# Blockwise attention with a routed MoE behind it: pages taken through the experts in an order found on the chip

## The chip, the cores and the metric

The kernel runs on 1 core of a Trainium2 chip. The metric is the device time of one execution in microseconds (us). One core has TensorE (PE, matrix multiplications; its weight loads are shown apart, as PEld), VectorE (DVE), ScalarE (ACT), GpSimd (POOL) and SyncE (SP, which here only issues transfers), each with its own instruction queue worked off in order, and 16 DMA engines that carry all transfers. SBUF is the memory the engines work on, PSUM the one that PE writes its results to.

## What is computed

Causal attention in blocks of 64, then a mixture of experts in which each token goes to one expert and no token is dropped:

```python
B, H, S, D = (8, 8, 576, 64)            # attention; x becomes N = 4608 rows of 512
N, D, E, F = (4608, 512, 8, 1024)       # MoE
...
scores = scale * np.matmul(q, k.transpose(0, 1, 3, 2))
mask = block_i >= block_j
attn = np.exp(scores - max) / sum
x = np.matmul(attn, v)                  # to [B * S, H * D]
...
expert_idx = np.argmax(x @ w_gate, axis=1)
gate_w = the softmax of x @ w_gate at expert_idx
for e in range(E):                      # the tokens of expert e
    y[e's tokens] = np.maximum(x[e's tokens] @ w1[e], 0.0) @ w2[e]
return gate_w[:, None] * y
```

The inputs are drawn at random from a fixed seed. How many tokens each expert gets is known only on the chip.

## The kernel before

**Attention** runs over 32 pairs of heads (`p`; four pairs are one batch `b`). The order of PE, ACT and POOL is written out by hand in the loop over `p`; DVE's and SP's order is found by the scheduler. A turn of the loop works on several pairs at once: POOL casts `q` and `k` of pair p+2 to 16 bits (`cast`), PE transposes them into the PSUM buffers `tp` (`trans`, L199, L201) and DVE copies them into `qkT` (L203, L205); PE makes the scores of pair p+1 (L230), ACT their exponentials `pt`; PE multiplies pair p's `pt` by `v` (`attend`, L261); DVE adds blocks of `pt` in `sums` (three instructions, the third is L243); PE makes the denominators (L284) and, in `finish`, transposes the result and multiplies it by the gate weights in one go (L304 with the denominators, L308), and DVE multiplies by the reciprocal into the rows `x16` and the logits `lgp` (L314 to L326). All transposes, denominators, finishes and the rank matmuls below share two PSUM buffers `tp`.

**Routing.** `route(b)` stands behind the finish of a batch's fourth pair. DVE sums the logits (L333), finds the largest and the one-hot `oh` of the expert (to L364); PE ranks the tokens in six matmuls (L367, L371), which stand in PE's queue directly behind finish; DVE then works out each token's row (`slot`) in `xsorted`, a table in DRAM of 43 pages of 128 rows, in which every page belongs to one expert (L378 to L409), and keeps count, pages in use and each expert's open page. `scatter(b, j)` writes a fifth of a batch's rows to their slots with an indirect DMA (L425), spread over the next batch's pairs. The weights (16 MB in fp16, `wall`) are loaded in 16 DMAs between pairs. `em_all` collects what is needed to say which expert each page has.

**Seam.** After the last route POOL issues five scatters, and DVE and PE work out `emap`, the expert of each of the 43 pages.

**MoE** goes through the pages in their order in the table. SP loads page T+4 (`mload`), PE reads the expert's number of that page into a register (`values_load`, L499). Per page PE does the first layer (`m1`, eight matmuls of 512 columns, L520, in which the register picks the weights), the transposes of the next page (`mtx`, four), those of the hidden layer of the page before (`mth`, eight, L532), and the second layer of the page before that (`m2`, eight matmuls, L542); DVE copies the transposes to SBUF, ACT applies relu and the gate, POOL writes the rows out with an indirect DMA (L546). The MoE's buffers are pools of their own, opened after those of attention are closed.

Of the kernel before, what the change touches and what calls it, by code (L numbers as in the profile page):

```python
# [22 lines left out]
def kernel(  # L23
# [69 lines left out]
    emap = consts.tile([1, NP], I32)  # L93
# [41 lines left out]
    with tc.tile_pool(name="ld", bufs=2) as ld, \  # L135
# [3 lines left out]
         tc.tile_pool(name="ptp", bufs=2) as ptp, \  # L139
# [4 lines left out]
         tc.tile_pool(name="t_ps", bufs=2, space=bass.MemoryType.PSUM) as t_ps:  # L144
# [186 lines left out]
        def route(b):  # L331
# [3 lines left out]
            x16 = st.pop(("x16", b))  # L335

            def small(name, w=E):
                return rp.tile([128, w], F32, name=name)

            def wide(name):  # L340
                return rp.tile([128, 5, E], F32, name=name)

            def over_j(t):
                return t.unsqueeze(1).to_broadcast([128, 5, E])

            def over_e(t):
                return t.unsqueeze(2).to_broadcast([128, 5, E])

# [4 lines left out]
            ex = wide("ex")  # L353
            nc.scalar.activation(ex, d, AF.Exp)
# [10 lines left out]
                                    in1=over_e(m2)[0:64, 4, :], op=ALU.is_equal)  # L365
            rk_ps = t_ps.tile([128, 6 * E], F32, name="tp")
# [54 lines left out]
        def scatter(b, j):  # L421

            slot, x16 = st["slot", b], st["x16", b]
            m = 128 if j < 4 else 64
            ins = nc.gpsimd.indirect_dma_start(  # L425
                out=xsorted[:, :],
                out_offset=bass.IndirectOffsetOnAxis(ap=slot[0:m, j:j + 1], axis=0),
                in_=x16[0:m, j, :], in_offset=None)
            apart("rows", ins)

        with tc.manual_schedule(engines={ET.PE, ET.Activation, ET.Pool}):
# [12 lines left out]
            for p in range(PAIRS):  # L444
# [13 lines left out]
                if p >= HP and p % HP < 3:  # L458
                    scatter(p // HP - 1, p % HP)
# [18 lines left out]
        for j in range(5):  # L478
            scatter(B - 1, j)
        with tc.manual_schedule(engines={ET.PE, ET.Activation}):  # L480
            em = rp.tile([128, 1], F32, name="em")
            nc.vector.reduce_sum(out=em, in_=em_all, axis=AX.X)
            em_ps = t_ps.tile([1, 128], F32, name="tp")
            nc.tensor.transpose(em_ps, em, ident32)
            nc.vector.tensor_scalar(emap, em_ps[:, 0:NP], -1.0, None, op0=ALU.add)
            nc.vector.tensor_single_scalar(emap, emap, E - 1, op=ALU.bitwise_and)  # L486

    with tc.tile_pool(name="xs", bufs=8) as xsp, \
         tc.tile_pool(name="m_sb", bufs=3) as m_sb, \
         tc.tile_pool(name="hp_ps", bufs=2, space=bass.MemoryType.PSUM) as hp_ps, \  # L490
         tc.tile_pool(name="yp_ps", bufs=2, space=bass.MemoryType.PSUM) as yp_ps, \
         tc.tile_pool(name="tt_ps", bufs=1, space=bass.MemoryType.PSUM) as tt_ps:
        pg = {}

        def mload(T):
            xs = xsp.tile([128, ROW], I32, name="xs")
            nc.sync.dma_start(out=xs, in_=xsorted[T * 128:T * 128 + 128, :])  # L497
            pg["xs", T] = xs
            pg["e", T] = nc.values_load(  # L499
                emap[0:1, T:T + 1], engines=[ET.PE], min_val=0, max_val=E - 1,  # L500
                skip_runtime_bounds_check_because="the low three bits of an integer")

        def mtx(T):
            ps = tt_ps.tile([128, 512], F16, name="xps")
# [10 lines left out]
        def m1(T):  # L515
            xT = pg.pop(("xT", T))
            hp = hp_ps.tile([128, F], F32, name="hp")
# [10 lines left out]
        def mth(T):  # L528
            h = pg.pop(("h", T))
            ps = tt_ps.tile([128, F], F16, name="hps")  # L530
            for f in range(8):
                nc.tensor.transpose(ps[:, f * 128:f * 128 + 128],  # L532
                                    h[:, f:F:8], ident16)
            hT = m_sb.tile([128, F], F16, name="hT")
            nc.vector.tensor_copy(hT, ps)  # L535
            pg["hT", T] = hT

        def m2(T):
            hT, xs = pg.pop(("hT", T)), pg.pop(("xs", T))
            yp = yp_ps.tile([128, Dm], F32, name="yp")  # L540
# [11 lines left out]
        with tc.manual_schedule(engines={ET.PE, ET.Activation}):  # L552
            for T in range(4):
# [43 lines left out]
```

## Time and profile before

| | |
|---|---|
| time, median of 3 runs | 531.01 us (529.99 to 533.31) |
| the profiled execution | 528.41 us |
| its span in the trace | 526.5 us |
| mean granted clock of TensorE | 0.933 |
| busy: PE, DVE, ACT, POOL | 446.2, 265.5, 205.9, 190.8 us |

The span runs from the first to the last instruction that the profiler recorded; 1.9 us of the execution's time lie around it. The views of the trace name an instruction by its line in the kernel (L520), its engine, its operation, and by tiles, "out<-in". In a timeline a row gives the start in us from the span's beginning, the duration, and in brackets how long the engine had been idle before and who released it; neighbours of one kind are drawn together (x8 is eight instructions). "issue" is idle time in which the engine waited for nothing that the profile shows. A granted clock of 1.00 is TensorE's full speed.

### The profile page before, as it was taken

Reading aid. Unit: us, or ns where it says so; the run is one execution under the profiler, and the core shown is the slowest. Engines: PE = TensorE matmul, PEld = TensorE weight load, DVE = VectorE, ACT = ScalarE, POOL = GpSimd, SP = SyncE. Lnnn points to the kernel's source line nnn. Section 1 sums busy time; section 2 is a strip of 40 time slices with the busy share of each in tenths; the row PEclk is TensorE's granted clock in tenths of the full one; section 3 lists DMA queues with packets and bytes.
Section 4 is the critical chain, followed back from the end, with each engine's and each line's share of the span. In section 5 each row is a group of like instructions: output and inputs, shape, how many; then the busy total and the mean of one; then the engine's idle time right before and its main releaser. Section 6 shows DMA issues by size and latency. Waiting matters only on the chain. (4 is left out here: it accounts for less than half of the span.)

```text
span 526.5 us, 11426 instructions
## 1 busy us (share of the span) xinstructions
PE 446.2 (85%) x4005; PEld 271.3 (52%) x4005; DVE 265.5 (50%) x745; ACT 205.9 (39%) x319; POOL 190.8 (36%) x379
## 2 busy tenths in 40 slices
PE   2996987896996996996996970699999999999991
PEld 1564655564664664664663650355555555555550
DVE  1567466778777677667867752122222222322220
ACT  2453443353453453452452520144334434434431
POOL 7433174354462463553552503022222222222221
PEclk9999899899898997997997995699999999999996
DMA  4689987678498586789585562212222232322200
GB/s 123 200 231 231 239 198 195 159 186 189 119 209 209 115 210 156 155 199 213 131 212 102 105 128 68 59 60 100 102 82 91 81 101 82 119 76 90 82 18 0
DMA packets 85589, 71.40 MB, mean 136 GB/s; under 512 B 52640, under 2 KB 80032, under 8 KB 83488
## 3 DMA queue, kind: packets, MB, share of 16 engines
q1 hardware_dynamic: 78000, 39.71, 28.9%
q0 software_dynamic: 7536, 30.98, 24.8%
q8 instruction: 34, 0.56, 0.4%
q14 instruction: 19, 0.16, 0.1%
HBM read 67.56 MB, written 21.71 MB: 170 GB/s over the span
## 5 line engine op out<-in xcount | busy, mean ns | idle before, releaser
L233 ACT ACTIVATE pt<-s 128x1024 f32<-128x1024 f32 x96 | 94.7, 1022 | 82.7 <-PE s L230 70.6
L261 PE MATMUL o<-pt,v 128*64 128x320 f32 (+3 forms) x768 | 102.6, 421 | 1.9 <-DMA v<-in_v_dram 1.9
L546 POOL DMA_INDIRECT out_dram<-y,xs x43 | 42.3, 984 | 149.8 <-ACT y L545 149.8
L509 DVE COPY xsT<-xps 128x512 f16<-128x512 f16 x43 | 18.3, 425 | 137.7 <-PE xps L506 95.8
L520 PE MATMUL hp<-wall,xsT 128*128 x344 | 83.0, 385 | 2.6 <-DVE xsT L509 2.6
L542 PE MATMUL yp<-wall,hT 128*128 x344 | 81.1, 379 | 0.0
L261 PEld LDWEIGHTS o<-pt,v 128*64 128x64 f32 x768 | 57.3, 152 | 44.5 <-issue 20.4
L203 DVE COPY qkT<-tp 128x512 f16<-128x512 f16 x64 | 43.9, 686 | 62.4 <-PE tp L201 55.9
L525 ACT ACTIVATE h<-hp 128x1024 f16<-128x1024 f32 x43 | 44.0, 1023 | 67.9 <-PE hp L520 66.8
L235 POOL MEMSET pt<- 64x128 f32 x128 | 23.6, 199 | 128.8 <-ACT pt L233 90.6
L187 POOL CAST qk<-qk 128x512 f16<-128x512 f32 x64 | 53.0, 851 | 12.8 <-DMA qk<-in_k_dram 6.2
L520 PEld LDWEIGHTS <-xsT 128*128 128x128 f16 x344 | 34.0, 99 | 43.8 <-issue 3.0
L308 PE MATMUL tp<-wgi,oT 128*128 128x144 f32 x320 | 55.0, 305 | 0.0
L425 POOL DMA_INDIRECT xsorted<-x,slot x40 | 41.5, 1038 | 34.2 <-DVE emap L486 14.2
L545 ACT ACTIVATE y<-yp,xs 128x512 f32<-128x512 f32 x43 | 29.5, 687 | 60.0 <-PE yp L542 60.0
L542 PEld LDWEIGHTS <-hT 128*128 128x128 f16 x344 | 32.2, 99 | 30.7
L265 ACT COPY oT<-o 128x256 f32<-128x256 f32 x64 | 25.7, 402 | 50.8 <-PE o L261 50.8
L308 PEld LDWEIGHTS tp<-wgi,oT 128*128 128x128 f32 x320 | 42.7, 190 | 2.9
L239 DVE TENSOR_TENSOR acc<-pt 128x896 f32<-128x896 f32 x32 | 35.0, 1092 | 18.0 <-issue 10.6
L230 PE MATMUL s<-qkT 64*128 64x512 f16 (+4 forms) x320 | 36.4, 321 | 2.5 <-DVE qkT L203 1.8
L535 DVE COPY hT<-hps 128x1024 f16<-128x1024 f16 x43 | 29.7, 692 | 7.8 <-PE hps L532 4.8
L199 PE MATMUL tp<-ident,qk 128*128 128x128 f16 x256 | 26.3, 227 | 8.0 <-POOL qk L187 8.0
(107 smaller groups left out, 489.6 us busy)
## 6 DMA issues: line engine op xcount, KB each, us to landing
wall<-in_moe_w_dram POOLq DMA_DIRECT2D x16, 1024.0 KB, 9.9
qk<-in_q_dram SPq DMA_DIRECT2D x32, 256.0 KB
qk<-in_k_dram SPq DMA_DIRECT2D x32, 256.0 KB
v<-in_v_dram SPq DMA_DIRECT2D x64, 128.0 KB
xs<-xsorted SPq DMA_DIRECT2D x43, 129.0 KB
xsorted<-fill SPq DMA_DIRECT2D x4, 516.0 KB
xsorted<-fill SPq DMA_DIRECT2D x3, 645.0 KB
xsorted<-fill SPq DMA_DIRECT2D x1, 1548.0 KB
```

Of the source, the lines that this page charges most:

```text
L187: nc.gpsimd.tensor_copy(h16[:, n, 0:4].rearrange("p c h d -> p h c d"), qk[:, n].rearrange("p h (c d) -> p h c d", c=4))
L203: nc.vector.tensor_copy(qkT[:, n, 0:512].rearrange("d (p c) -> d p c", c=4), ps[:, 0:512].rearrange("d (c p) -> d p c", c=4))
L230: nc.tensor.matmul(out=sp[:, h, o:o + w], lhsT=qkT[r, 1, c * 128:c * 128 + 128], rhs=qkT[r, 0, q0:q0 + w], start=True, stop=True)
L233: nc.scalar.activation(pt[:, :, t * 512:t * 512 + 512], sp, AF.Exp, scale=scale)
L239: nc.vector.tensor_tensor(out=acc[:, :, 0:448], in0=pt[:, :, 128:576], in1=pt[:, :, 576:1024], op=ALU.add)
L261: nc.tensor.matmul(out=o[h * 64:h * 64 + 64, q0 - lo:hi - lo], lhsT=vt[r, c, h, :], rhs=src, start=(c == 0), stop=(c == last), skip_group_ ...
L308: nc.tensor.matmul(out=ps[:, m * 144:m * 144 + 144], lhsT=oT[:, i * 128:i * 128 + 128], rhs=wgi[:, hp, :], start=True, stop=True, skip_gro ...
L425: ins = nc.gpsimd.indirect_dma_start(out=xsorted[:, :], out_offset=bass.IndirectOffsetOnAxis(ap=slot[0:m, j:j + 1], axis=0), in_=x16[0:m, ...
L520: nc.tensor.matmul(out=hp[:, half * 512:half * 512 + 512], lhsT=xT[:, c * 128:c * 128 + 128], rhs=weight(T, 2 * c + half), start=(c == 0), ...
L525: nc.scalar.activation(h, hp, AF.Relu)
L542: nc.tensor.matmul(out=yp, lhsT=hT[:, f * 128:f * 128 + 128], rhs=weight(T, 8 + f), start=(f == 0), stop=(f == 7))
L546: ins = nc.gpsimd.indirect_dma_start(out=out[:, :], out_offset=bass.IndirectOffsetOnAxis(ap=xs[:, 257:258], axis=0), in_=y, in_offset=None ...
```

## The change

The change has three parts.

- **Routing is split.** `choose(b)`, DVE's part up to `oh`, stays behind finish. `route(b)` (the exponential on ACT, the rank matmuls on PE and the rest of DVE's work) moves into the next pair, between its last scores and its denominators. Scatters move with it, two in each of the next two pairs' turns and one in the third; batch 6's fifth goes out after the loop.
- **The order of the pages.** After batch 6 `closed` marks the pages that are full, or whose expert has gone on to another page. `first_places` and `orders` number them with matmuls against a triangle of ones and put the first ten of them, page numbers and experts, into `order1`. The other 33 places get their pages in `order2`; their experts are known when batch 7 is routed (`last_experts`, `last_order`).
- **MoE begins before batch 7 is routed.** Its PSUM buffers are those of attention (`s`, `o0`, `o1`, `tp`), its SBUF buffers take the place of `pt`. Loads of the first ten places don't wait for batch 7's scatters. SP reads the page's number into a register for each load and runs five places ahead; PE reads the expert's number in `mtx`, one page ahead. `route(7)`, its scatters and the last experts stand behind m1 of place 1, `last_order` behind m1 of place 3.

```diff
-        def route(b):
+        def choose(b):
             lg = rp.tile([128, 5, E], F32, name="lg")
...
+            st["d", b] = d
+
+        def route(b):
+            d, x16, oh = st.pop(("d", b)), st.pop(("x16", b)), ohs[b % 2]
+            ex = wide("ex")
+            nc.scalar.activation(ex, d, AF.Exp)
             rk_ps = t_ps.tile([128, 6 * E], F32, name="tp")
...
+        def closed():
+            cur, hit = small("cur"), small("hit")
+            opn, cl = small("opn", 1), small("cl", 1)
+            nc.vector.scalar_tensor_tensor(out=cur, in0=lastA, scalar=-1.0, in1=pages,
+                                           op0=ALU.add, op1=ALU.add)
+            nc.vector.tensor_scalar(hit, cur, page_f, 0.0, op0=ALU.is_equal, op1=ALU.add,
+                                    accum_out=opn)
+            nc.vector.scalar_tensor_tensor(out=cl, in0=page_f, scalar=used, in1=opn,
+                                           op0=ALU.is_lt, op1=ALU.is_gt)
...
+        def orders():
+            on, fst, rest, em_h = st.pop("first")
+            ps = t_ps.tile([128, 3 * FIRST], F32, name="tp")
+            nc.tensor.matmul(out=ps[0:1, 0:FIRST], lhsT=page_h, rhs=on, start=True, stop=True,
+                             skip_group_check=True)
+            nc.tensor.matmul(out=ps[0:1, FIRST:2 * FIRST], lhsT=em_h, rhs=on, start=True,
+                             stop=True, skip_group_check=True)
...
+            nc.vector.tensor_copy(order1, ps[0:1, 0:2 * FIRST])
...
-                if p >= HP and p % HP < 3:
-                    scatter(p // HP - 1, p % HP)
+                if p > HP and p % HP > 0 and nxt:
+                    scatter(p // HP - 1, 2 * (p % HP - 1))
...
+                if p > HP and 0 < p % HP < 3:
+                    scatter(p // HP - 1, 2 * (p % HP) - 1)
                 if p > 2 and (p - 3) * 16 // 29 != (p - 4) * 16 // 29:
                     load_weights((p - 3) * 16 // 29)
+                if p >= HP and p % HP == 0:
+                    route(p // HP - 1)
+                if p == PAIRS - 3:
+                    first_places()
+                if p == PAIRS - 2:
+                    orders()
                 denominators(p)
                 finish(p, 1)
                 finish(p, 0)
-                if p >= HP and p % HP < 2:
-                    scatter(p // HP - 1, 3 + p % HP)
                 if p % HP == HP - 1:
-                    route(p // HP)
...
+                    choose(p // HP)
+                if p == PAIRS - 4:
+                    closed()
+
+        scatter(B - 2, 4)
+        probs.close()
+        xsp = moe.enter_context(tc.tile_pool(name="xs", bufs=8, reuse_waits="tile"))
+        m_sb = moe.enter_context(tc.tile_pool(name="m_sb", bufs=2, reuse_waits="tile"))
...
         def mload(T):
             xs = xsp.tile([128, ROW], I32, name="xs")
-            nc.sync.dma_start(out=xs, in_=xsorted[T * 128:T * 128 + 128, :])
+            page = number(T, 0, ET.SP, NP - 1)
+            ins = nc.sync.dma_start(
+                out=xs, in_=xs_pages[:, ds(page, 1), :].rearrange("p a r -> p (a r)"))
+            if T < FIRST:
+                tc.declare_no_dep(ins.ins, group="last rows", reason="pages closed before")
             pg["xs", T] = xs
-            pg["e", T] = nc.values_load(
...
         def mtx(T):
...
             pg["xT", T] = xT
+            pg["e", T] = number(T, 1, ET.PE, E - 1)
...
             for T in range(NP + 2):
-                if T + 4 < NP:
-                    mload(T + 4)
                 if T < NP:
                     m1(T)
+                if T == 1:
+                    route(B - 1)
+                    for j in range(5):
+                        scatter(B - 1, j)
+                    last_experts()
+                if T == 3:
+                    last_order()
+                if T + 5 < NP:
+                    mload(T + 5)
                 if T + 1 < NP:
                     mtx(T + 1)
```

Where instructions stand on an engine, before and after (each row is the line, the operation, and the tiles with the shape; an `x2` is two in a row).

On PE, before, at the end of a batch's fourth pair (here batch 0): finish, the ranks, and the next pair's scores.

```order
L308 MATMUL tp<-wgi,oT_167 128x144 x2
L304 MATMUL tp<-sel,den_171 128x10
L308 MATMUL tp<-wgi,oT_167 128x144 x3
L367 LDWEIGHTS before_76
L367 MATMUL tp<-oh_174,before_76 128x40
L371 LDWEIGHTS ones_78
L371 MATMUL tp<-oh_174,ones_78 128x40
...
L371 MATMUL tp<-oh_174,ones_78 128x8
L230 LDWEIGHTS qkT
L230 MATMUL s<-qkT 128x512
```

On PE, after, the same ranks, in the pair that follows: they stand behind that pair's last scores (L234) and ahead of its denominators (L295).

```order
L234 LDWEIGHTS qkT
L234 MATMUL s<-qkT 64x64
L380 LDWEIGHTS before_76
L380 MATMUL tp<-oh_182,before_76 128x40
L384 LDWEIGHTS ones_78
L384 MATMUL tp<-oh_182,ones_78 128x40
...
L384 MATMUL tp<-oh_182,ones_78 128x8
L295 MATMUL tp<-pt,picks 32x128
L295 MATMUL tp<-acc,picks 32x128
```

The six rank matmuls have moved back by most of a pair: a whole pair's scores, products with `v` and transposes now stand between finish and them.

On DVE, before, at the same place: the last instruction of the one-hot (L364), then the rest of route, from the copy of the ranks (L378) to the slots (L409), and the next copies into `qkT` (L203, L205).

```order
L362 TENSOR_TENSOR oh_174<-val,m_721 128x32
L364 TENSOR_TENSOR oh_174<-val,m_721 64x8
L376 RECIPROCAL x_365<-sm 128x5
L378 COPY rk<-tp 128x48
L382 TENSOR_TENSOR cnt_737<-cnt,rk 128x8
L400 TENSOR_TENSOR w_757<-rk,room 128x40
...
L407 TENSOR_REDUCE sl<-w_757 128x5
L409 CAST slot<-sl 128x5
L203 COPY qkT<-tp 128x512
L205 COPY qkT<-tp 128x64
```

On DVE, after, behind the one-hot (L371): the copies into `qkT` (L214, L216) of the next turn, then the rest of route (from L391 on), in between the sums (L250, L252, L254).

```order
L371 TENSOR_TENSOR oh_182<-val,m_727 64x8
L214 COPY qkT<-tp 128x512
L216 COPY qkT<-tp 128x64
L214 COPY qkT<-tp 128x512
L216 COPY qkT<-tp 128x64
L391 COPY rk<-tp 128x48
L395 TENSOR_TENSOR cnt_824<-cnt,rk 128x8
...
L401 TENSOR_TENSOR new<-pages_825,pages 128x8
L250 TENSOR_TENSOR acc<-pt 128x2x448
L402 SCALAR_TENSOR_TENSOR inc<-ione,used,new 128x8
L252 TENSOR_TENSOR acc<-acc,pt 128x2x320
L403 TENSOR_TENSOR base<-inc,new 128x8
```

The copies stand directly behind choose now; the rest of route stands behind them, and the next pair's sums stand among it.

On PE, before, in a late page: the last matmul of a second layer (L542), then the next page's first layer (L520), with the load of an expert's number (L499) behind its first weight load.

```order
L542 LDWEIGHTS hT
L542 ISA
L542 MATMUL yp<-wall,hT 128x512
L520 LDWEIGHTS xsT
L499 TENSOR_LOAD emap
L520 ISA
L520 MATMUL hp<-wall,xsT 128x512
```

On PE, after, in a late page: the load (L582) stands behind the next page's transposes (L598) and the first weight load of the hidden layer's transposes (L625).

```order
L598 LDWEIGHTS xs
L598 MATMUL o_5701<-ident_69,xs 128x128
L625 LDWEIGHTS h_5643
L582 TENSOR_LOAD order_124
L625 MATMUL o_5711<-ident_69,h_5643 128x128
L625 LDWEIGHTS h_5643
L625 MATMUL o_5711<-ident_69,h_5643 128x128
```

The load has moved past the first layer's eight matmuls and the four transposes, ahead of the eight transposes of the hidden layer.

## Rows read from the trace of the kernel before

**Rows 1.** Windows: stretch, us, busy PE, PEld, DVE, ACT, POOL; PEclk; DMA share; GB/s

```profile
20.00:47.10 27.10, 26.51 (x314) 17.58 (x311) 18.43 (x41) 13.94 (x25) 11.04 (x25) 1.00 0.90 255
93.00:280.60 187.60, 162.09 (x1750) 105.44 (x1750) 138.33 (x412) 81.84 (x145) 91.54 (x181) 0.92 0.76 175
200.00:210.00 10.00, 5.62 (x43) 3.61 (x42) 8.93 (x42) 2.87 (x7) 3.83 (x7) 0.69 0.57 151
345.00:500.00 155.00, 155.00 (x1041) 85.39 (x1039) 41.30 (x74) 63.77 (x75) 36.40 (x37) 1.00 0.27 91
```

**Rows 2.** Waits: who waited for whom, us in total, times, longest us

```profile
PE tp L367 <- DVE oh L364: 33.7, 8, 4.4
...
PE xps L506 <- issue: 11.9, 1, 11.9
...
PE tp L284 <- DVE qkT L205: 1.3, 5, 0.4
```

**Rows 3.** Timeline, PE, round the route of batch 4: start us, duration, instruction

```profile
200.89 0.29 PE L304 MATMUL tp<-sel,den 128*128 128x10 f32 x2
...
206.40 0.22 PE L367 MATMUL tp<-oh,before 128*128 128x40 f16 x1 [4.38 <-DVE oh L364]
...
207.63 4.31 PE L261 MATMUL o<-pt,v 128*64 128x256 f32 x24
...
215.25 0.29 PE L304 MATMUL tp<-sel,den 128*128 128x10 f32 x2
...
216.84 2.81 PE L261 MATMUL o<-pt,v 128*64 128x256 f32 x24
...
223.05 0.29 PE L304 MATMUL tp<-sel,den 128*128 128x10 f32 x2
```

**Rows 4.** Timeline, PE: the longest wait for `v`

```profile
82.39 3.21 PE L261 MATMUL o<-pt,v 128*64 128x256 f32 x24 [1.57 <-DMA v<-in_v_dram]
```

**Rows 5.** Timeline, PE: end of attention, first pages, one late page

```profile
310.94 0.98 PE L308 MATMUL tp<-wgi,oT 128*128 128x144 f32 x6
...
332.27 3.57 PE L520 MATMUL hp<-wall,xsT 128*128 x8 [1.02 <-DVE xsT L509]
...
344.63 1.89 PE L520 MATMUL hp<-wall,xsT 128*128 x8
...
348.81 1.89 PE L520 MATMUL hp<-wall,xsT 128*128 x8
...
490.72 1.89 PE L520 MATMUL hp<-wall,xsT 128*128 x8
```

**Rows 6.** Timeline, DVE, round the same route

```profile
202.57 0.78 DVE L243 TENSOR_TENSOR acc<-acc,pt 128x384 f32<-128x384 f32 x1
...
204.39 0.72 DVE L333 TENSOR_REDUCE lg<-lgp 128x40 f32<-128x320 f32 x1
...
206.19 0.15 DVE L364 TENSOR_TENSOR oh<-val,m 64x8 f16<-64x8 f32 x1
...
206.77 0.21 DVE L378 COPY rk<-tp 128x48 f32<-128x48 f32 x1 [0.33 <-PE tp L371]
...
209.84 0.17 DVE L409 CAST slot<-sl 128x5 int32<-128x5 f32 x1
...
216.73 1.91 DVE L243 TENSOR_TENSOR acc<-acc,pt 128x384 f32<-128x384 f32 x1
...
220.50 0.69 DVE L203 COPY qkT<-tp 128x512 f16<-128x512 f16 x1 [0.85 <-PE tp L201]
```

**Rows 7.** Timeline, POOL, the casts beside the sum of 216.73

```profile
216.71 1.17 POOL L187 CAST qk<-qk 128x512 f16<-128x512 f32 x2
```

**Rows 8.** DMA issues: count, KB each, median us from issue to landing

```profile
wall<-in_moe_w_dram POOLq DMA_DIRECT2D x16, 1024.0 KB, 9.9
...
xsorted<-x,slot POOLq DMA_INDIRECT x40, 3.1
```

**Rows 9.** Line 499: loads of the expert number: ns min/median/max, first and last start

```profile
L499 PEldq TENSOR_LOAD <-emap x43: 297/558/804, 328.9 to 489.2; - x43
```

More of the change, by code (lines that the diff above doesn't have):

```diff
@@ new lines, in experts, with first_places @@
+        def experts():
+            em = small("em", 1)
+            nc.vector.reduce_sum(out=em, in_=em_all, axis=AX.X)
+            em_i = rp.tile([128, 1], I32, name="em_i")
+            nc.vector.tensor_scalar(em_i, em, -1.0, None, op0=ALU.add)
+            nc.vector.tensor_single_scalar(em_i, em_i, E - 1, op=ALU.bitwise_and)
+            em_h = rp.tile([128, 1], F16, name="em_h")
+            nc.vector.tensor_copy(em_h, em_i)
+            return em_h
+        def first_places():
+            cl, cl16 = st.pop("closed")
+            ps = t_ps.tile([128, 1], F32, name="tp")
+            nc.tensor.matmul(out=ps, lhsT=before16, rhs=cl16, start=True, stop=True)
+            at, fst = small("at", 1), small("fst", 1)
+            nc.vector.scalar_tensor_tensor(out=at, in0=cl, scalar=-1024.0, in1=ps,
+                                           op0=ALU.mult, op1=ALU.add)
+            nc.vector.tensor_scalar(at, at, 1024.0, None, op0=ALU.add)
+            on = consts.tile([128, FIRST], F16)
+            nc.vector.tensor_scalar(on, place[:, 0:FIRST], at, None, op0=ALU.is_equal)
+            nc.vector.tensor_single_scalar(fst, at, float(FIRST), op=ALU.is_lt)
+            rest = consts.tile([128, 1], F16)
+            nc.vector.tensor_scalar(rest, fst, -1.0, 1.0, op0=ALU.mult, op1=ALU.add)
+            st["first"] = on, fst, rest, experts()
@@ new lines, in orders @@
+        def orders():
[5 more added lines that the diff above has]
+                             stop=True, skip_group_check=True)
+            nc.tensor.matmul(out=ps[:, 2 * FIRST:2 * FIRST + 1], lhsT=before16, rhs=rest,
+                             start=True, stop=True, skip_group_check=True)
+            nc.vector.tensor_copy(order1, ps[0:1, 0:2 * FIRST])
+            at = small("at2", 1)
+            nc.vector.scalar_tensor_tensor(out=at, in0=fst, scalar=1024.0,
+                                           in1=ps[:, 2 * FIRST:2 * FIRST + 1],
+                                           op0=ALU.mult, op1=ALU.add)
+            on2 = consts.tile([128, NP - FIRST], F16)
+            nc.vector.tensor_scalar(on2, place[:, 0:NP - FIRST], at, None, op0=ALU.is_equal)
+            st["second"] = on2
@@ new lines, in last_experts, with last_order @@
+        def last_experts():
+            st["em_h"] = experts()
+        def last_order():
+            on2 = st.pop("second")
+            n = NP - FIRST
+            ps = t_ps.tile([1, 2 * n], F32, name="tp")
+            nc.tensor.matmul(out=ps[:, 0:n], lhsT=page_h, rhs=on2, start=True, stop=True,
+                             skip_group_check=True)
+            nc.tensor.matmul(out=ps[:, n:2 * n], lhsT=st["em_h"], rhs=on2, start=True, stop=True,
+                             skip_group_check=True)
+            nc.vector.tensor_copy(order2, ps)
@@ L473 @@
                 finish(p, 0)
-                if p >= HP and p % HP < 2:
-                    scatter(p // HP - 1, 3 + p % HP)
                 if p % HP == HP - 1:
-                    route(p // HP)
[L478 to L486, printed above, removed]
@@ new lines, with number @@
+        probs.close()
+        xsp = moe.enter_context(tc.tile_pool(name="xs", bufs=8, reuse_waits="tile"))
+        m_sb = moe.enter_context(tc.tile_pool(name="m_sb", bufs=2, reuse_waits="tile"))
+        pg = {}
+        def number(T, what, engine, top):
+            t, n, at = (order1, FIRST, T) if T < FIRST else (order2, NP - FIRST, T - FIRST)
+            return nc.values_load(
+                t[0:1, what * n + at:what * n + at + 1], engines=[engine], min_val=0,
+                max_val=top, skip_runtime_bounds_check_because="each place has one page")
@@ L552 @@
         with tc.manual_schedule(engines={ET.PE, ET.Activation}):
-            for T in range(4):
+            for T in range(5):
                 mload(T)
```

55 lines of the change are left out of this document (30 added, 25 removed).

## The prediction, made before the changed kernel was run

> **What bounds the kernel now.** I read four views in this order: the windows by stage, the waits, the timelines round one route, and the timeline of the seam between attention and MoE. The windows [rows 1] show two regimes. From 345 us on TensorE (PE) is busy 155.00 of 155.00 us at a granted clock of 1.00: the MoE stage has nothing to win but a shorter start. In attention (93 to 280.6 us) it is busy 162 of 187.6 us, at a mean clock of 0.92, and the DMA engines are 0.76 busy. The list of waits [rows 2] says where the missing time is: the matmul that ranks the tokens (line 367) waited 33.7 us in 8 waits, up to 4.4 us each, for VectorE's (DVE's) one-hot `oh`; and the first transposes of MoE (line 506) waited 11.9 us once. One plain wait of the denominators for the copy of line 205 recurs (5 times, at most 0.4): that copy ends just when PE wants it, so DVE has no slack there, though it is half idle.
>
> Around one route [rows 3]: the denominator matmul of line 304 marks each pair of heads. From 200.89 to 215.25 is 14.36 us, from there to the next 7.80. The excess, 6.56, is the wait of 4.38 and a slow stretch: the 24 matmuls of line 261 took 4.31 us against 2.81 in the next pair (1.50), and the window 200 to 210 has a granted clock of 0.69 [rows 1], a mix of its two levels (1.00 is 2.4 GHz, 0.50 is 1.2). What is left, 0.7, are the rank matmuls (I put them at 0.3) and the scores behind them at the low clock. So the wait costs 4.38 and then about 1.9 more. A wait of 1.57 us, for `v` at 82.39 [rows 4], is followed by matmuls at 3.21, near the quick ones. There are seven such pairs inside attention, of 14.0 to 14.4 us; the eighth route stands in the seam.
>
> At the seam [rows 5], PE ends its last finish at 310.94 + 0.98 = 311.92 (call it E). The first MoE matmul starts at 332.27 and takes 3.57 where later pages take 1.89; page 3 starts at 344.63, and from there pages follow each other at 4.18 (348.81 − 344.63). So page 3 starts at E + 32.7.
>
> **Routes inside attention.** The change splits a route in two. `choose` (lg to oh) stays behind finish, on DVE alone; rank matmuls and the rest go into the next pair, between its scores and its denominators. So PE no longer stops for oh: 6.56 goes, and DVE's time comes in its place. Choose took from 204.39 to 206.34 = 1.95 us, the rest from 206.77 to 210.01 = 3.24 [rows 6]. In a plain pair DVE then sits idle 0.85 before the copies into `qkT` (the row at 220.50) [rows 6]. Choose now stands before those copies: they come 1.95 − 0.85 = 1.1 late. The rank matmul needs a PSUM buffer that the first copy frees, so it waits about 0.95; it takes 0.3; the denominators wait for the second copy's buffer. Worked through, this pair is about 1.7 longer. The rest of route (3.24, plus two instructions for the sum of `ex`, 0.2 each) is spread between the sums and the multiplications of that pair, where DVE idles at most some 2 us a pair, and it delays the next copies by 0.45 to 1.65; I take 0.8. The excess becomes 2.5 (bounds 2.2 and 3.4), with no wait over 1.6 us and hence no slow clock. The gain is 6.56 − 2.5 = 4.1 a route; the ends are 3.2 and 4.4, or 6.56 if DVE hid all of it.
>
> **DMA.** It must keep up. A batch holds 0.76 × 187.6 / 5 = 28.5 us of DMA work in 37.5 us [rows 1]; with 4.1 less it would be 28.5 / 33.4 = 0.85. Early it is fuller (0.90 from 20 to 47.1), and there PE already waits for loads [rows 1, 4]. So I count 5 × 4.1 = 20.5 for the later five routes less 2 for loads that come late, and for the first two 4 of 8.2 (ends 1 and 8). Attention: −22.5. Its own ends: −46 (seven times 6.56, nothing added) and −10.
>
> **The cast beside DVE.** While POOL (GpSimd) casts, twice in 1.17 us from 216.71 [rows 7], DVE's third sum (line 243) took 1.91 us, against 0.78 in the pair before [rows 6]: 1.1 more. Route's rest has a dozen instructions with two SBUF inputs, as that sum has, and now runs in pairs with casts; before, it ran with POOL idle. If each route is held up once more in this way, that is 7 × 1.1 = 7.9; the lower end is 0. I take 0, since the instructions are of 0.2 us and can be held between casts at little loss, and keep the other end as a rival. The Trainium skill, page "SBUF — State Buffer", section "Who interferes with whom", states that a DVE instruction with two SBUF inputs contends with a GpSimd one that reads SBUF, and that the one that comes second is blocked for the whole of the other; this row agrees (1.1 more beside casts of 0.6 each). By that rule the sum would stand at its other end.
>
> **The seam.** Ten pages that no later batch can reach are loaded while the last pair still runs, so MoE can start behind E. After E, DVE needs its reciprocal, four multiplications and the copy xsT(0), so m1(0) starts at about E + 2.2; by the rows, from the end of the third sum (203.35) to choose (204.39) took the multiplications 1.04 [rows 6]. Choose(7), 1.95, then stands ahead of xsT(1): m1(1) at E + 5; the rank matmuls 0.4 and a copy, m1(2) at E + 8.5; then the transposes and m2(0), 2.4 in all, and m1(3) at about E + 13.1, all at full clock since no wait passes 2.2. The two order matmuls add 0.3. The gain is 32.7 − 13.4 = 19.3 (ends 15 and 21). The loads have time: page 0 is asked for, at the latest, when batch 6's last scatter has landed (3.1 us from issue [rows 8]), which POOL issues ahead of the last weight load. The last expert's weights decide too: 9.9 us to landing [rows 8], issued in pairs 29 (w1) and 31 (w2): w1, for m1(0), has landed by E; w2 is needed by m2(0) at E + 10, and lands before that. Batch 7's scatters go out by E + 20 and have landed by E + 23, page 10 is needed at about E + 40.
>
> **Added work.** POOL makes a few more constants ahead of the first cast (estimate 0.5 by its neighbours), `closed`, `first_places` and `orders` put about 20 small DVE instructions of about 0.2 [rows 6] into pairs 28 to 30, mostly hidden: 0.5. Ends 0 and 3. Each page now needs a register load of its expert in a new place on PE, and SP (SyncE) a register load and an address per page. SP's run five pages ahead, over 20 us, so I cost them at nothing. PE's: before, 43 loads of 0.558 (up to 0.804), the last at 489.2 [rows 9], while the matmuls ahead of which it stands began at 490.72 [rows 5]. So PE's instruction queue ran 1.5 us ahead of the array, and with PE never idle [rows 1] the loads cost nothing. Now the load stands behind four short transposes instead of eight long matmuls. The same count of instructions ahead is worth only 0.9 to 1.1 us there: four transposes and three or four matmuls of m1 of 0.22. That still exceeds 0.56; the cover is thin. Bounds: 0, and 43 × 0.558 = 24.
>
> The Trainium skill, page "DMA: Bandwidth & Descriptors", section on latency and other measured facts, gives a register load from memory (`tensor_load`) a floor of about 600 ns; the rows here go down to 297, so the measurement decides. By the page's figure the bound would be 26.
>
> **Sum.** The profiled execution took 528.41 (span 526.5 and 1.9 around it): 528.4 − 22.5 − 19.3 + 1.0 = 487.6. The median of the three runs shown is 531.01, 2.6 above; on that footing the sum is 490.2. I forecast 489.0.
>
> **Rivals.**
> - *DVE and DMA hide everything*: attention −46, 528.4 − 46 − 19.3 + 1 = 464. For it: DVE is idle half the time. Against: the copies have no slack. 0.10.
> - *DMA becomes the bound*: if it can't exceed a mean share of 0.80, a batch takes 28.5 / 0.80 = 35.6, five gain 1.9 each, the first two nothing: 528.4 − 9.5 − 19.3 + 1 = 500.6. For it: early pairs wait for loads. Against: 0.90 was held from 20 to 47.1. 0.18.
> - *Casts hold up route's rest* (above): 487.6 + 7.9 = 495.5. For it: the one sum of 1.91. Against: instructions of 0.2 us lose little. 0.10.
> - *The expert load shows on PE*: some 0.3 to 0.56 a page, 13 to 24 in all: 501 to 512. 0.09.
> - *The early start doesn't happen*: the first ten loads wait for batch 6's last scatter or for the SBUF they take from `pt`, and come late; the seam then gains about 5: 502. 0.05.
> - *Slower*: the scatter of a batch's last 64 rows now goes out one pair before `x16` of the batch after next is claimed by POOL's iota, behind a 1 MB weight load (9.9 us). If it lands late, POOL stops, with the casts behind it, then PE. Slack is about 11 us (one pair and most of the next); the price is whatever passes it, once a batch. From 41 / 7 = 5.8 us late per batch, landing 17 us after issue, all is given back, beyond 6.6 the kernel is slower: 535 at 7. Against: a scatter lands in 3.1, a weight load in 9.9 [rows 8]. 0.02.
>
> **Chances and range.** The forecast's case gets 0.46. Its own range is 479 to 497 (excess 2.2 to 3.4, the first two routes 1 to 8, seam 15 to 21). Rival two, the scatter of the early start and half of the expert load are taken in above, and half of the first rival below: 470 to 506. A measurement of this kernel tells about 1% (5.3 us) from no change. All cases but the slower one and the far end of the expert load are more than 1% faster: 0.95 faster, 0.03 within 1%, 0.02 slower.
>
> **What would show it.** Right: line 304 of route pairs 10 to 10.5 us apart; waits of the rank matmul near 1 us; clock 1.00 there; the first MoE matmul within 3 us of the last finish; pages 4.18 apart. Wrong: pages over 4.3 apart (expert load); pairs without a route over 8 us with PE waiting for `v` or the casts (DMA); casts or sums of 2 us and more in route pairs (casts beside DVE); a gap over 4 us at the seam; POOL idle before its iota.

## The result, and the profile after

The changed kernel took 486.55 us (median of 4 runs, 485.14 to 491.17), the kernel before 531.63 beside it: a ratio of 0.917, 95% interval 0.910 to 0.924. Here and below a median is over all executions of a kernel, and a ratio leaves out those over 1.5% above its fastest. The forecast was 489.0, in a range of 470 to 506. The profiled execution took 486.03, with a span of 484.2 us, 42.3 less than before. Where it came from is read off two points. The last finish ends at 285.70 + 0.98 = 286.68 instead of 311.92: attention is 25.2 shorter. From there to the end of the span are 197.5 us instead of 214.6: the seam is 17.1 shorter. The forecast had 21.5 (22.5 less 1.0 for added work) and 19.3.

PE's timeline of the changed kernel, with the numbers of its own lines: L315 is the denominator matmul that marks a pair, L380 the first rank matmul, L295 denominators, L272 products with `v`, L474 the matmul of `first_places`, L613 a page's first layer.

```profile
105.65 0.29 PE L315 MATMUL tp<-sel,den 128*128 128x10 f32 x2
...
152.92 0.29 PE L315 MATMUL tp<-sel,den 128*128 128x10 f32 x2
...
159.14 0.19 PE L380 MATMUL tp<-oh,before 128*128 128x40 f16 x1 [0.27 <-DVE qkT L216]
...
159.92 0.27 PE L295 MATMUL tp<-pt,picks 128*32 128x128 f32 x1 [0.48 <-DVE rk L391]
...
161.54 0.29 PE L315 MATMUL tp<-sel,den 128*128 128x10 f32 x2
...
169.44 0.29 PE L315 MATMUL tp<-sel,den 128*128 128x10 f32 x2
...
242.55 0.29 PE L315 MATMUL tp<-sel,den 128*128 128x10 f32 x2
...
247.39 2.81 PE L272 MATMUL o<-pt,v 128*64 128x256 f32 x22 [2.60 <-DMA v<-in_v_dram]
...
253.50 0.29 PE L315 MATMUL tp<-sel,den 128*128 128x10 f32 x2
...
262.12 0.29 PE L315 MATMUL tp<-sel,den 128*128 128x10 f32 x2
...
268.74 0.18 PE L474 MATMUL tp<-cl,before 128*128 128x1 f16 x1 [0.67 <-DVE qkT L216]
269.53 0.37 PE L295 MATMUL tp<-pt,picks 128*32 128x128 f32 x1 [0.61 <-DVE em_i L465]
...
272.43 0.44 PE L315 MATMUL tp<-sel,den 128*128 128x10 f32 x2
...
285.70 0.98 PE L319 MATMUL tp<-wgi,oT 128*128 128x144 f32 x6
...
289.13 2.71 PE L613 MATMUL s<-wall,xsT 128*128 x8 [2.23 <-DVE lg L356]
...
293.30 3.57 PE L613 MATMUL s<-wall,xsT 128*128 x8 [1.02 <-DVE xsT L601]
...
302.05 1.89 PE L613 MATMUL s<-wall,xsT 128*128 x8
...
306.48 1.89 PE L613 MATMUL s<-wall,xsT 128*128 x8
...
460.92 1.89 PE L613 MATMUL s<-wall,xsT 128*128 x8
...
462.87 0.66 PE L625 MATMUL o<-ident,h 128*128 128x128 f16 x8
```

A pair with a route now takes 161.54 − 152.92 = 8.62 instead of 14.36 [rows 3], and the next 7.90. The two waits that are left, 0.27 and 0.48, stand where 4.38 stood. Pairs are counted from 0; a pair without a route commonly takes 7.71. Two such pairs run long: pair 27, 242.55 to 253.50 (10.95), with a wait of 2.60 for `v`, and pair 29, 262.12 to 272.43 (10.31), which carries `closed` and `first_places`. Page 3 starts at 302.05, E + 15.4, against E + 32.7 [rows 5]; from 306.48 to 460.92 are 37 pages, 4.17 each, as before.

The windows of the changed kernel (columns as in [rows 1]):

```profile
20.00:47.10 27.10, 26.52 (x312) 17.32 (x308) 18.14 (x41) 13.67 (x24) 10.84 (x24) 1.00 0.97 250
93.00:260.00 167.00, 157.02 (x1778) 106.29 (x1776) 132.15 (x419) 82.59 (x147) 93.88 (x181) 1.00 0.89 201
245.00:250.00 5.00, 2.61 (x22) 2.16 (x22) 0.91 (x4) 1.40 (x3) 2.03 (x5) 1.00 0.93 242
267.50:270.00 2.50, 1.22 (x22) 0.84 (x24) 2.46 (x17) 1.14 (x2) 2.12 (x4) 0.91 0.48 124
270.00:272.50 2.50, 2.50 (x25) 1.95 (x18) 1.42 (x3) 0.27 (x1) 1.57 (x2) 0.50 0.64 146
291.00:296.00 5.00, 3.98 (x13) 1.60 (x12) 0.42 (x1) 1.02 (x1) 0.00 (x0) 0.50 0.01 4
300.00:450.00 150.00, 150.00 (x1006) 82.46 (x1005) 41.40 (x87) 61.54 (x72) 39.62 (x41) 1.00 0.29 94
```

In attention the mean clock has gone from 0.92 to 1.00 and the DMA share from 0.76 to 0.89: five batches' transfers now pass in 167.0 us instead of 187.6. MoE is still 150.00 of 150.00 busy. Two stretches at 0.50 (1.2 GHz) are new: 270 to 272.5 and 291 to 296. The waits:

```profile
POOL qk L198 <- DMA qk<-in_q_dram: 11.6, 4, 7.7
...
PE o L272 <- DMA v<-in_v_dram: 5.9, 3, 2.6
...
PE tp L295 <- DVE rk L391: 2.9, 6, 0.5
...
PE s L613 <- DVE lg L356: 2.2, 1, 2.2
...
PE tp L380 <- DVE qkT L216: 1.3, 5, 0.3
```

The ranks' 33.7 us of waiting [rows 2] have become 1.3, and 2.9 of the denominators behind them; the waits for loads (`v` for PE, `q` for the casts) are the longest that remain inside attention.

### The profile page after: what moved, and what is told of

Read it like the earlier page. It is cut to its first block, busy times and chain, and to the rows that moved or that the text cites. A ratio compares the mean times of both kernels' runs of the same rounds, so it can differ in the third digit from the quotient of the medians.

```text
span 484.2 us, 11576 instructions
## 1 busy us (share of the span) xinstructions
PE 440.9 (91%) x4010; PEld 272.7 (56%) x4010; DVE 258.1 (53%) x764; ACT 205.3 (42%) x319; POOL 194.8 (40%) x383
## 4 chain that ended last, share of the span: by engine, by line
issue 29%; POOL 9%; DMA 7%; PE 6%; DVE 4%; SPq 2%; POOLq 1%; DVEq 0%
POOL out_dram L639 9%; DMA v<-in_v_dram 5%; PE o L272 2%; DMA xs<-xsorted 2%; PE tp L319 1%; PE tp L295 1%; POOL xsorted L438 1%; DVE qkT L214 1%; POOLq L639 1%; DVE acc L250 1%; PE s L241 0%; SPq L589 0%; SPq L191 0%; DVE acc L252 0%; SPq L179 0%
## 5 line engine op out<-in xcount | busy, mean ns | idle before, releaser
L272 PE MATMUL o<-pt,v 128*64 128x320 f32 (+3 forms) x768 | 95.8, 394 | 6.0 <-DMA v<-in_v_dram 5.9
L639 POOL DMA_INDIRECT out_dram<-y,xs x43 | 42.3, 985 | 125.1 <-ACT y L638 124.5
L613 PE MATMUL s<-wall,xsT 128*128 x344 | 83.8, 387 | 3.4 <-DVE lg L356 2.2
L635 PE MATMUL tp<-wall,hT 128*128 x344 | 81.1, 379 | 0.0
L601 DVE COPY xsT<-o 128x512 f16<-128x512 f16 x43 | 18.2, 424 | 115.7 <-PE o L598 115.5
L272 PEld LDWEIGHTS o<-pt,v 128*64 128x64 f32 x768 | 56.0, 141 | 41.7 <-issue 11.2
L214 DVE COPY qkT<-tp 128x512 f16<-128x512 f16 x64 | 43.7, 683 | 50.6 <-PE tp L212 50.6
L618 ACT ACTIVATE h<-s 128x1024 f16<-128x1024 f32 x43 | 44.1, 1025 | 54.0 <-PE s L613 54.0
L438 POOL DMA_INDIRECT xsorted<-x,slot x40 | 47.3, 1182 | 32.7 <-DVE em_h L467 20.2
L198 POOL CAST qk<-qk 128x512 f16<-128x512 f32 x64 | 50.7, 812 | 23.3 <-DMA qk<-in_q_dram 11.6
L613 PEld LDWEIGHTS <-xsT 128*128 128x128 f16 x344 | 34.1, 99 | 44.8 <-issue 3.2
L638 ACT ACTIVATE y<-tp,xs 128x512 f32<-128x512 f32 x43 | 29.6, 689 | 60.8 <-PE tp L635 60.8
L276 ACT COPY oT<-o 128x256 f32<-128x256 f32 x64 | 25.7, 402 | 46.6 <-PE o L272 46.6
L250 DVE TENSOR_TENSOR acc<-pt 128x896 f32<-128x896 f32 x32 | 35.9, 1121 | 13.5 <-issue 7.6
L241 PE MATMUL s<-qkT 64*128 64x512 f16 (+4 forms) x320 | 33.9, 303 | 2.5 <-DVE qkT L214 1.8
L628 DVE COPY hT<-o 128x1024 f16<-128x1024 f16 x43 | 29.7, 691 | 7.6 <-PE o L625 4.8
```

The costliest lines, as they stand in the source:

```text
L198: nc.gpsimd.tensor_copy(h16[:, n, 0:4].rearrange("p c h d -> p h c d"), qk[:, n].rearrange("p h (c d) -> p h c d", c=4))
L214: nc.vector.tensor_copy(qkT[:, n, 0:512].rearrange("d (p c) -> d p c", c=4), ps[:, 0:512].rearrange("d (c p) -> d p c", c=4))
L241: nc.tensor.matmul(out=sp[:, h, o:o + w], lhsT=qkT[r, 1, c * 128:c * 128 + 128], rhs=qkT[r, 0, q0:q0 + w], start=True, stop=True)
L250: nc.vector.tensor_tensor(out=acc[:, :, 0:448], in0=pt[:, :, 128:576], in1=pt[:, :, 576:1024], op=ALU.add)
L272: nc.tensor.matmul(out=o[h * 64:h * 64 + 64, q0 - lo:hi - lo], lhsT=vt[r, c, h, :], rhs=src, start=(c == 0), stop=(c == last), skip_group_ ...
L438: ins = nc.gpsimd.indirect_dma_start(out=xsorted[:, :], out_offset=bass.IndirectOffsetOnAxis(ap=slot[0:m, j:j + 1], axis=0), in_=x16[0:m, ...
```

## The experiments

Each was timed beside the kernel before. Where kernels of different series are compared, it is by the ratio to that.

**One half of the change at a time.** The first kernel takes the kernel before and only splits and moves the routes; the second takes the changed kernel and puts the seven inner routes and their scatters back.

```diff
 # first, in the kernel before
+                if p >= HP and p % HP == 0:
+                    route(p // HP - 1)
                 denominators(p)
...
-                    route(p // HP)
+                    choose(p // HP)
 # second, in the changed kernel
                     choose(p // HP)
+                    if nxt:
+                        route(p // HP)
```

> The kernel before with the routes split and moved into the next pair, and nothing else: pages in the old order, MoE behind the last route. If the two halves of the change add up, this has all of the attention's gain and none of the seam's: the last finish came at 286.68 in the changed kernel and at 311.92 before, 25.2 earlier, so 531.6 - 25.2 = 506 (504 to 509; the lower end if the small matmuls of the page order, absent here, were what lengthened pair 29 by 2.6). Rival: the attention's gain hangs on the seam (loads of the first pages, SP's order), then it differs from 506 by over 4.

> The changed kernel with the seven routes inside attention and their scatters put back behind finish; the order of pages and the early start stay. If the halves add up: the seam's gain alone, 214.6 - 197.5 = 17.1, so 531.6 - 17.1 = 514.5 (512 to 517). Rival: the early start needs the split (pages ready later, scatters late), then the seam gains under 14 and the time is over 517.

Measured: 496.29 (ratio 0.931, 0.925 to 0.938) and 513.40 (0.968, 0.963 to 0.973). The second is as expected. The first is some 10 better than expected: over 4 from 506, which is what its rival named, that the two halves do not act alone. PE's timeline of the split alone, its last finish and page 3:

```profile
279.99 0.98 PE L308 MATMUL tp<-wgi,oT 128*128 128x144 f32 x6
...
313.12 1.89 PE L526 MATMUL hp<-wall,xsT 128*128 x8
```

Its seam is the old one (page 3 at E + 32.1), but E is 280.97, 5.7 earlier than in the changed kernel. So the split alone is worth 30.9, and the changed kernel lost 5.7 of it. In that kernel pairs 29 and 30, without the page order, take 7.8 and 6.9 instead of 10.3 and 7.4 (3.0). The rest lies in pairs that wait for loads: 1.4 in pair 20 (184.92 to 194.94 in the changed kernel), 1.0 in pairs 4 and 5, 0.3 in pair 7. Pair 20 takes 8.62 in the next two kernels below, which have the same attention, so at least this 1.4 belongs to one execution and not to the change. The seam's gain stands by itself; inside attention the page order takes back 3.0 of the split's, or 1.5 where the clock does not fall, as in the kernel with three register loads.

**Keeping PE busy at the seam.**

```diff
             mtx(0)
+            spin(10)      # matmuls of 512 columns into a spare s buffer
             for T in range(NP + 2):
+                if T == 1:
+                    spin(4)
                 if T < NP:
                     m1(T)
```

> The changed kernel with matmuls whose result nobody reads: ten of 512 columns ahead of the first page's first layer, four ahead of the second's. Theory: the seam fell short of the forecast by 2.3 because the granted clock fell to 0.50 from 291 to 296; with PE kept busy m1 of pages 0 and 1 take 1.89 each instead of 2.71 and 3.57, and the register load of page 0 is hidden: 2.5 to 3.5 off, 483 to 484. Rival: the seam is bound by the chain over DVE (choose ahead of the copy), then the clock is full but the time stays within 1 of 486.5.

Measured: 480.62 (0.906, 0.900 to 0.911). PE's timeline, and the window over the seam:

```profile
283.76 0.98 PE L319 MATMUL tp<-wgi,oT 128*128 128x144 f32 x6
...
286.96 1.89 PE L613 MATMUL s<-wall,xsT 128*128 x8
...
290.01 1.89 PE L613 MATMUL s<-wall,xsT 128*128 x8
...
297.06 1.89 PE L613 MATMUL s<-wall,xsT 128*128 x8
```

```profile
286.00:298.00 12.00, 11.81 (x81) 6.33 (x79) 7.52 (x45) 3.88 (x5) 0.98 (x1) 1.00 0.23 67
```

At a clock of 1.00 both first layers take 1.89, and page 3 starts at 297.06, E + 12.3 (E = 284.74) instead of E + 15.4: 3.1 off, as the theory had it: 2.5 in the two first layers, the rest in earlier starts. The rival, that the chain over DVE alone made the seam longer than forecast, falls; the chain itself remains, and the added matmuls fill it. The rest of the difference lies in attention, whose late pairs differ from run to run (E was 286.68 there).

**Three register loads a page.**

> The changed kernel with three register loads of the expert number per page on PE instead of one (the first two are not used). Theory of the prediction: the cover at the new place is 0.9 to 1.1 us, so one load of 0.56 is hidden and three (1.7) stick out by 0.6 to 0.8 a page: +25 to +34, 511 to 520, and pages 4.8 to 5.0 apart. Rival: the queue runs further ahead (1.5 us and more, as it did before) and the time stays within 8 of 486.5.

Measured: 483.56 (0.911, 0.905 to 0.917). The experiment failed: of the loads whose value nobody uses none was issued, as line 582 shows.

```profile
L582 PEldq TENSOR_LOAD <-order x43: 297/301/483, 283.8 to 456.4; - x43
```

There are 43 loads, not 129. The cover has to be read from the changed kernel itself (below), and how many loads it would hide stays untested. What this kernel does show, being nearly the changed one, is how far attention's late pairs move: pair 27 takes 9.91 in it, 10.95 in the changed kernel and 13.99 in the one with the busy seam.

**What makes pairs late.** Six kernels change the DMA work. In the first, every second weight load is left out.

```diff
-                    load_weights((p - 3) * 16 // 29)
+                    if (p - 3) * 16 // 29 % 2 == 0:
+                        load_weights((p - 3) * 16 // 29 // 2)
```

> The changed kernel with half of the weights left out: only every second of the 16 loads of 1 MB is issued, and the expert numbers are taken modulo 4. Theory: the pairs that run long without a route (47.76 to 72.91 takes 25.15 for two, of which one has a route; 242.55 to 253.50 takes 10.9) wait for loads that are late behind DMA work; with 8 MB less they come down to 7.7, 8.6 with a route: 4.6 + 4.2 + 3.2 and part of 184.92 to 194.94 (1.4) off, about 12: 473 to 477. Rival: they come from SP's own order or from the casts, and the time stays within 3 of 486.5.

Measured: 478.42 (0.898, 0.894 to 0.903). The late pairs in the second half are gone (239.56 to 247.38 is 7.8), but in the first half one of 16.5 us remains, with a wait of 6.5 for `v`. So the weights explain the later ones and not the first, and the time lies between theory and rival.

> The changed kernel with the fills of the page table (5.7 MB, in the first four pairs) spread up to pair 21. Theory: the two early long pairs (25.15 together) are late because fills and the first weight loads meet there; spread, they fall to 17 to 20: 5 to 8 off, 479 to 482. Rival: the DMA engines are so full that the work only moves, and later pairs get longer by as much: within 2 of 486.5.

Its edit asks for a pair of its own for each of the eight fills, 0, 2, 5, 9, 11, 13, 17 and 21, but SP's order is found by the scheduler. In the trace SP has issued all eight by 78.2 us, in pair 7, and twice two at once:

```profile
50.44 4.59 SPq L127 DMA_DIRECT2D xsorted<-fill  x2
...
76.16 2.07 SPq L127 DMA_DIRECT2D xsorted<-fill  x2
```

Measured: 485.89 (0.915, 0.911 to 0.919), the rival's number. The jam moved from pairs 4 and 5, which take 8.6 and 8.9 here, to pair 7 (72.94 to 88.54, 15.6):

```profile
79.82 5.41 PE L273 MATMUL o<-pt,v 128*64 128x256 f32 x24 [5.23 <-DMA v<-in_v_dram]
```

Since the fills were not spread up to pair 21, this does not decide between theory and rival.

Next, the weights in 32 loads of 0.5 MB, one a pair (two in pairs 3, 12 and 22); then the same with the seam kept busy.

```diff
-        e, part = n // 2, n % 2
+        e, part, a = n // 4, n // 2 % 2, n % 2
...
+                    for n in range(((p - 3) * 32 + 28) // 29, ((p - 2) * 32 + 28) // 29):
+                        load_weights(n)
```

> The changed kernel with the same weights loaded in 32 DMAs of 0.5 MB, one a pair, instead of 16 of 1 MB every other pair. Theory: pairs are late because a 1 MB burst meets the loads of q, k and v, not because the sum of the DMA work is too large; smoothed, the long pair 27 (10.9) falls to 7.8 and the two early ones (25.15) lose 3 to 5: 6 to 8 off, 478 to 481. Rival: what counts is the total (share 0.89), then the lateness only moves: within 2 of 486.5.

> The same with the matmuls that keep PE busy at the seam (run before: 3.0 off in the seam). If bursts count: 475 to 478. Rival: 483 to 484, the seam's part alone.

Measured: 480.29 (0.905, 0.902 to 0.907) and 477.72 (0.900, 0.897 to 0.903). Both beat the changed kernel beyond the intervals, and the second is the fastest whole kernel here, 52.5 under the kernel before. In the first, every pair from 81 us on is now 7.7 to 8.6, except pair 29 (9.1) and the last two, which are shorter (7.1 and 5.8). PE waits for no load there, though the DMA share is higher than in the changed kernel (0.93 against 0.89) and the total of the weights is the same:

```profile
93.00:260.00 167.00, 159.60 (x1836) 106.17 (x1834) 136.64 (x439) 84.41 (x152) 105.54 (x200) 1.00 0.93 201
```

So for the later pairs the size of one burst counts, and not the total. The two early pairs did not follow the theory: they take 25.7 together, against 25.15, and nearly all of the excess is now in one, 56.36 to 73.61; SP's queue ahead of it, then PE:

```profile
47.45 2.90 SPq L127 DMA_DIRECT2D xsorted<-fill  x3
...
51.37 5.71 SPq L188 DMA_DIRECT2D v<-in_v_dram  x1
```

```profile
65.56 4.55 PE L269 MATMUL o<-pt,v 128*64 128x256 f32 x24 [7.54 <-DMA v<-in_v_dram]
```

Three fills go out at once, beside the two weight loads of pair 3, and behind them SP stands 5.71 us in one issue that commonly takes 0.6. Two attempts to take the fills away from there:

> The same again with the fills of the page table spread, two pages a pair from pair 3 to 18, issued by POOL behind the weight load. If bursts count: the early pairs fall to 8.6 and 7.8 and the time to 470 to 474. Rival: POOL's scatters now wait for a fill of the pair before to land, the casts stand behind them, and the time is over 484.

> The kernel with half loads and the matmuls at the seam, with the eight fills issued by SP one at a time, in pairs 0, 1, 3, 6, 9, 12, 15 and 18, and SP's order written out like that of the other queues, so that no two fills go out together. Theory: the one long pair left in it (55.62 to 74.49, 18.8) waits for v behind three fills issued at once with two weight loads; without that it takes 8 to 11: 468 to 471. Rival: any fill beside the other loads jams the queue for a pair, wherever it stands, and the time stays at 476 to 479 or rises.

Measured: 493.95 (0.931, 0.928 to 0.934) and 492.24 (0.927, 0.924 to 0.930), slower than the kernel with half loads and the busy seam by 16 and 14.5. In both that pair falls to its length without a jam (56.25 to 64.26 in the second), with the weight loads where they were, so the jam needs the three fills. But fills that come after the first scatter are waited for by the scatters behind them. POOL in the second:

```profile
75.66 1.01 POOL L436 DMA_INDIRECT xsorted<-x,slot  x1 [7.57 <-DMA xsorted<-fill]
```

POOL stands there, and with it the casts and then PE; its scatters waited 23.4 us for fills in 3 waits, and 44.1 in 10 in the first. So for the first of the two the rival held, with its mechanism and its number (over 484). For the second the time rose, as the rival said, but not by its mechanism: PE waits for no `v` in the whole kernel, so the jam did go, and a new wait cost more.

**The page order in pair 29.**

```diff
                 attend(p, (2, 3, 4), 1)
+                if p == PAIRS - 3:
+                    first_places()
...
-                if p == PAIRS - 3:
-                    first_places()
```

> The changed kernel with first_places moved in PE's order ahead of the transposes of pair 29. Theory: pair 29 (262.12 to 272.43, 10.3) is long because first_places takes a turn in the two tp buffers between the transposes and the denominators (waits of 0.67 and 0.61) and the clock then fell to 0.50: it comes down to 7.7 to 8.3, 2.0 to 2.6 off, 484 to 484.5. Rival: the 20 small DVE instructions are what delays it, and it stays at 9 to 10.3.

Measured: 487.11 (0.916, 0.911 to 0.921). The pair stayed at 10.5: the matmul now waits 1.2 for `em_i` instead, and DVE is busy without a gap from 264 to 270. The rival holds: DVE has the rest of route(6), `closed` and `first_places` in that pair. Each alone costs little there: pair 29 takes 7.79 in the kernel with the split alone, and 8.41 in the one with the early start alone, whose route(6) is done before. Keeping the seam busy, the fills of the earlier edit and this one together:

> The three edits together: matmuls that keep PE busy at the seam, fills spread, first_places early. If they add up: 486.5 - 3 - (5 to 8) - 2 = 473 to 477, faster than the changed kernel and the kernel before. Rival: DMA lateness moves to other pairs, then 480 to 482.

Measured: 485.16 (0.907, 0.902 to 0.911); by the ratio some 482, the rival's number. The seam keeps its gain (page 3 starts at 302.44, E + 12.4), but the fills stand in SP's queue as in the kernel above, and PE waits 5.9 us for `v` in pair 7, which takes 16.1. The edits don't add up.

## Why the prediction was right, point by point

Of the signs that the prediction named for being right, the clock of 1.00, the first MoE matmul 2.45 after the last finish and the pages 4.17 apart came. Two did not: route pairs are 8.6 apart and not 10 to 10.5, and the ranks wait 0.27 and not near 1. A sign of being wrong came too: pairs without a route over 8 us in which PE waits for `v`.

**The wait that bounds.** Right: the ranks' wait and the clock behind it were what a route cost. With them gone the clock of attention is 1.00.

**The excess of a route pair** was mis-sized: forecast 2.5, measured 8.62 − 7.71 = 0.9 and 0.1 to 0.6 in the next pair, 1.1 together on the five later routes. The step that failed is "they come 1.95 − 0.85 = 1.1 late". The 0.85 was read in a pair in which the third sum had been held to 1.91 by the casts [rows 6]; DVE's slack without that is about 2 (0.85 and the 1.1 that the sum had lost; the row of 150.37 shows 2.13 in a pair ahead of the route), as much as choose takes. DVE around the route of the timeline above, and POOL:

```profile
150.37 0.69 DVE L214 COPY qkT<-tp 128x512 f16<-128x512 f16 x1 [2.13 <-PE tp L212]
...
152.25 1.09 DVE L250 TENSOR_TENSOR acc<-pt 128x896 f32<-128x896 f32 x1 [0.40 <-issue]
...
156.42 0.74 DVE L356 TENSOR_REDUCE lg<-lgp 128x40 f32<-128x320 f32 x1
...
158.31 0.68 DVE L214 COPY qkT<-tp 128x512 f16<-128x512 f16 x1
...
160.89 1.54 DVE L250 TENSOR_TENSOR acc<-pt 128x896 f32<-128x896 f32 x1
...
162.35 0.57 DVE L402 TENSOR_TENSOR_SCAN inc<-ione,used,new 128x8 f32<-128x8 f32 x1
```

```profile
160.88 2.02 POOL L198 CAST qk<-qk 128x512 f16<-128x512 f32 x2
```

The copies start 5.39 after the pair's mark (152.92), against 5.25 before (220.50 − 215.25): 0.14 late, not 1.1. The rank matmul then waits 0.27 (forecast 0.95) and the denominators 0.48.

**The cast beside DVE.** The mechanism is there: the first sum took 1.54 (1.09 at 152.25) and a small scan 0.57 (0.23 before) beside the casts, and the two casts took 2.02, against 1.17 [rows 7]. Little of it reaches PE: the next pair is 7.90, 0.2 over a plain one. The end taken, 0, was nearly right, and the rival, with 1.1 a route, falls. The Trainium skill, "SBUF — State Buffer", section "Who interferes with whom", states that a DVE instruction with two SBUF inputs contends with a GpSimd one that reads SBUF; the trace agrees on the blocking (1.54 against 1.09 for the same sum), and shows that it costs PE 0.2 at most here.

**DMA** was right in kind, and larger than the 2 us counted. The first two routes gained 5.1 (pair 9 is marked at 105.65 now), 4 forecast. Before, it was

```profile
110.72 0.29 PE L304 MATMUL tp<-sel,den 128*128 128x10 f32 x2
```

From there to E attention fell from 201.2 to 181.0: 20.2, where the forecast had 20.5 less 2 for loads and 1 for added work. Over pairs of 7.71 the five later routes cost 33.2 before and 5.3 now, a gain of 27.9. Of it 7.7 were lost again: 3.2 and 1.4 in pairs 27 and 20, with waits of 2.60 and 0.97 for `v`, and 2.6 and 0.5 in pairs 29 and 30, with the page order. The excess of a route and the losses were each off by a factor of two or more, in opposite directions: a gain per route too small by 1.5 (5.6 against 4.1, 7.4 for five) and losses too small by 4.7. That most of the one was cancelled by the other, and that the 3.7 by which attention gained more met 2.2 less at the seam, is luck: the time came within 1% of the forecast, its terms did not. The rival in which the DMA engines stop at a share of 0.80 falls; they went to 0.89.

**Added work.** 0.5 for the page order was mis-sized: pair 29 alone lost 2.6, half of it to the clock, and pair 30 another 0.5. The same pair with the same two waits took 9.0 in the kernel with the busy seam, where the clock stayed at 1.00:

```profile
270.00:272.50 2.50, 2.50 (x25) 1.93 (x26) 2.28 (x4) 0.46 (x2) 1.28 (x2) 1.00 0.70 126
```

**The seam.** Forecast 19.3, measured 17.1. The step that failed is "all at full clock since no wait passes 2.2": m1 of pages 0 and 1 ran at 2.71 and 3.57 instead of 1.89, 2.5 in all, and keeping PE busy gave 3.1 back. No row carried that step: the waits read before were 1.57, with the clock kept, and 4.38, with the clock lost; this one was 2.23. The rest (m1(0) at E + 2.45, scatters, weights, loads of the first ten pages) came as worked out.

**The register load.** Hidden, as costed, but the cover was mis-sized. In the changed kernel:

```profile
L582 PEldq TENSOR_LOAD <-order x43: 296/300/483, 288.4 to 460.5; - x43
```

The last load starts at 460.5, the transposes ahead of which it stands at 462.87: the queue is 2.4 us ahead there, not 0.9 to 1.1. The load itself took 0.300 instead of 0.558 [rows 9]; why it became shorter no run here shows. The Trainium skill, "DMA: Bandwidth & Descriptors", section on latency and other measured facts, puts a floor of about 600 ns on a `tensor_load`; 43 loads at 0.3 differ from it, and the measurement decides.

**The slower rival** didn't occur in the changed kernel, but the two kernels with late fills show its mechanism at full price: a scatter that waits on POOL for a write to land holds the casts, and PE with them, and gave back some 15 us. Its price of 535 at 7 us late is a slip: 487.6 and seven times 7 are 536.6.

## What to carry to other kernels

Work taken off the critical engine's queue is worth the wait plus what the clock loses behind it (here 4.38 and about 1.9), but the pace then passes to whatever shares the new period, here the DMA engines. Their share does not tell by itself whether a load will be late: 0.89 on average held a wait of 2.6 for `v`, and 0.93 with smaller loads held none. Break large background loads into pieces of one period (16 of 1 MB to 32 of 0.5 MB took 6 us off), and don't put a transfer behind which others must wait into the stretch where those others run. A slack read from one period holds only if that period had nothing else stretched in it.

## What was not expected of the hardware

- The length of an idle stretch alone did not tell whether the clock fell. A wait of 2.60 at 247.39 left the granted clock at 1.00 (245 to 250, PE busy 2.61 of 5); two waits of 0.67 and 0.61 (267.5 to 270, PE busy 1.22 of 2.5) were followed by 0.50, and the same two waits in the kernel with the busy seam and in the one of the register loads were not (pair 29 took 9.03 and 9.02). What tells these apart stays open.
- One SP issue of a 16 KB load took 5.71 us behind three fills (commonly 0.6), at a DMA share of 1.00 from 47 to 56 us: here a full DMA shows up as a long issue on the queue as well as a late landing.
- The jams differ between executions of the same attention: in the changed kernel and the two next to it (busy seam, register loads) pair 27 took 10.95, 13.99 and 9.91, and pair 20 took 10.02, 8.62 and 8.63.
